# Second-level sums by accumulating DMAs, and a longer lead for loads and splits in the last phase of a Fourier-mixing and gated feed-forward kernel

## The chip, the cores and the metric

The kernel runs on one core of a Trainium2 chip. The metric is the time of one execution on the device in microseconds, the median over several runs; lower is better. The engines are named as in the profile: PE multiplies matrices, PEld loads its weights, DVE and ACT work on vectors, POOL and SP here issue DMAs, and 16 DMA engines move the data.

## The reference, cut to what matters

```python
# x: 1 x 2048 x 640 (S x D); the DFT matrices are 2048 x 2048 and 640 x 640;
# W_gate, W_up: 640 x 1728; W_down: 1728 x 640; all float32
xn = (x - mean(x)) / sqrt(var(x) + 1e-5)                    # over D
a, b = xn @ dft_hid_re.T, xn @ dft_hid_im.T
fnet = dft_seq_re @ a - dft_seq_im @ b
h = relu(xn @ W_gate) * (xn @ W_up)
out = x + fnet + h @ W_down
```

## The kernel before, in words

Every float32 operand is split into a high part of type fp32r and the low remainder, and each product is three matmuls: high times high, high times low, low times high (`mm3`, lines 138 to 140 on PE). A split is two instructions, a copy to the high part on ACT (line 132) and a subtraction on DVE (line 133). To save matmuls, large products are cut into 2 x 2 blocks and done in seven products with sums of blocks (the scheme of Strassen and Winograd).

The kernel has three stages. The first takes the DFT along the sequence, with the matrices streamed in. The second, of 26 steps, makes gate and up, multiplies them, and stores the result `h` in DRAM (`hd`; `hr` is its last 64 rows). Beside that, `pair_weights` prepares the weights of the third stage: it reads two blocks of rows of the hidden DFT matrix or of W_down, makes sums and differences, splits some of them, and POOL stores them in DRAM (`wparts`, `wquads`). The last PE work of this stage is a lead unit on the tile `gw`.

The third stage, `project`, adds both products of the hidden dimension into the output tiles `y`: once for the half q=1 of the sequence, then for q=0. Its unit is one pair (or two) of row blocks times weights. In order, the names of the products are B11, T1, T2, B22 (first part), T3, B22 (rest), T4, with two short B21 units inside T4. Beside them runs a second level (`second_level`) on a part of the output that falls out of the scheme: seven quad products named 1, 2, 5, 6, 3, 7, 4, each over three groups of operands, so 21 quad units. The names 5, 6, 7 and 4 use sums of two blocks.

A unit has steps: `load` (DMAs on SP), `prepare` (sums and splits on DVE and ACT), `run` (PE) and `read` (PE's banks into `y`, on DVE). `drive(4, 2)` walks the list of units: at position i it prepares unit i-2, loads unit i, reads out unit i-5 and runs unit i-4. The order on SP, POOL and PE in this stage is the order of the code; DVE and ACT are ordered by the scheduler. Tiles come from pools with a fixed number of buffers: a DMA into a buffer waits on its queue until the last reader of what stood there before, in this pool or in the space of an earlier one, is done, and all DMAs behind it on that queue wait too.

Names in rows: `rw` and `ro` are blocks of rows of an operand, `wr` is raw weights, `wt` split weights, `cb` a split operand, `q` the second level's operands, `ps` a bank of PE's results, `pq` and `hd` operands in DRAM, `in_hid` and `in_wd` the weights as given.

Of the kernel before, what the change touches and what calls it, by code (L numbers as in the profile page):

```python
# [12 lines left out]
P = 128  # L13
# [18 lines left out]
BACK = 3  # L32

# [20 lines left out]
Z1, Z4, HIGH, LOW, Y21, Y11, Y12 = (2 * P * i for i in (0, 1, 2, 5, 8, 9, 10))  # L54
Z2, Z3, Y22 = (2 * P * i for i in range(3))
NW = 16 * P


QUAD_LOW, QUAD_HIGH, NPREP = 16 * P, 20 * P, 24 * P
QUADS = ((0, 2), (1, 3), (KD, KD + 2), (KD + 1, KD + 3), (KD + 4, KD + 5))  # L60
GROUPS = (("hid", 0, 2, 0), ("f", 0, 2, 2), ("f", 4, 1, 4))
PREP_ORDER = (0, 2, 1, 3, 4, 5, 7, 6, 8, 9, 10)
# [3 lines left out]
def fnet_reglu_kernel(  # L66
# [41 lines left out]
    wquads = dram_p.tile([P, len(QUADS), 4, 2, P], F32, name="wquads")  # L108
# [917 lines left out]
    made = {}  # L1026

    def pair_weights(k, n):

        t = {}  # L1030
        quad = next((i for i, (_, second) in enumerate(QUADS) if second == k), None)

        def load():
            made[k] = t["z"] = z = pool("prep").tile([P, NPREP], F32, name="pw")
            wa, wb = pair(k, 1)
            for w, o1, o2 in ((wa[0], Y11, Y21), (wb[0], Y12, LOW + Y22)):
                rows = slice(0, w.shape[0])
                nc.sync.dma_start(z[rows, o1 : o1 + 2 * P], w[:, : 2 * P])
                nc.sync.dma_start(z[rows, o2 : o2 + 2 * P], w[:, 3 * P :])

        def prepare():
            z = t["z"]
            zz = lambda b: z[:, b : b + 2 * P]
            if k == ODD:
                for o in (Y12, LOW + Y22):
                    nc.vector.memset(z[REST:, o : o + 2 * P], 0.0)
# [7 lines left out]
            if quad is not None:  # L1054
                halves = [[w[:, Y12 + i * P : Y12 + (i + 1) * P] for i in range(2)] for w in (made[QUADS[quad][0]], z)]
                (a11, a21), (a12, a22) = halves
                s1, s2, s3, s4 = (z[:, QUAD_LOW + i * P : QUAD_LOW + (i + 1) * P] for i in range(4))
                minus = lambda o, i0, i1: nc.vector.scalar_tensor_tensor(o, i0, -1.0, i1, op0=OP.mult, op1=OP.subtract)
                tt(s1, a22, a21, op=OP.subtract)
                minus(s2, s1, a11)  # L1060
                tt(s3, a11, a21, op=OP.subtract)
                minus(s4, a12, s2)
                low = z[:, QUAD_LOW:QUAD_HIGH]
                split(z[:, QUAD_HIGH:NPREP].bitcast(F32R), low, low)

        def keep():
            z = t["z"]
            nc.gpsimd.dma_start(wparts[:, k], z[:, :NW])
            if quad is not None:
                for v, at in enumerate((QUAD_HIGH, QUAD_LOW)):  # L1070
                    nc.gpsimd.dma_start(wquads[:, quad, :, v], z[:, at : at + 4 * P].rearrange("p (s n) -> p s n", s=4))

        loads[n - 1].append(load)
        besides[n].append(prepare)
        issues[n + 1].append(keep)

# [43 lines left out]
    for i, k in enumerate(PREP_ORDER):  # L1120
        pair_weights(k, 13 + i)
# [27 lines left out]
    for n, b, side in (("wraw", 4, "left"), ("ring2", 3, "left"), ("wts", 5, "left"), ("raws", 20, "left"),  # L1149
# [6 lines left out]
    SINGLE = (2, ODD_AT)  # L1156
    every = range(len(UNITS))
    fixed = [bank() for _ in range(8)]
# [33 lines left out]
    def project(q):  # L1192
# [3 lines left out]
        B = {("a", 0): A[0], ("a", 1): A[1], ("b", 0): Bk[0], ("b", 1): Bk[1], ("c", 0): Bk[0], ("c", 1): Bk[1],  # L1196
             "v1": fixed[7 if q else 4], "v2": fixed[4], "v3": fixed[4]}
# [20 lines left out]
        def unit(name, u, first, last):  # L1218
# [6 lines left out]
            weights = lambda: pool("wts").tile([P, 2, 2, 3 * P], F32R, name="wt")[:, :n]  # L1225

            def load():
                if name == "B11" and (q, u) == (1, 0):
                    return
                kind = {"B11": "B11", "T1": "B12", "T3": "B21"}.get(name)  # L1230
                if kind:
                    get(kind, u)
# [3 lines left out]
                if name == "B11" and ("B11", 0) not in raws:  # L1236
                    get("B11", 0)
                own, sums = [i.rearrange("k p n -> p k n") for i in pair(k0, n)], wparts[:, k0 : k0 + n]
                if short:
                    t["r"] = r = pool("wraw").tile([P, 2, 3 * P], F32, name="wr")[:, 0]  # L1240
                    for at in (upper, lower):
                        if name == "B22":
                            nc.sync.dma_start(r[at, :P], own[1][:, 0, 2 * P : 3 * P])
                            nc.sync.dma_start(r[at, P:], sums[:REST, 0, Z4 : Z4 + 2 * P])
                        else:
                            cs = slice(0, 3 * P) if name == "B21" else slice(3 * P, D)
                            nc.sync.dma_start(r[at, : cs.stop - cs.start], own[1][:, 0, cs])
                    return
                if name in PARTS:
                    t["w"] = w = weights()  # L1250
                    for j in range(n):
                        at = sums[:, j, HIGH:].rearrange("p (v n) -> p v n", v=2)[:, :, PARTS[name] : PARTS[name] + 2 * P]
                        nc.sync.dma_start(w[:, j, :, : 2 * P].bitcast(F32), at)
                    return
                t["r"] = r = pool("wraw").tile([P, 2, 3 * P], F32, name="wr")[:, :n]
                if name in ("B11", "B21"):
                    nc.sync.dma_start(r, own[name == "B21"][:, :, : 3 * P])
                else:
                    z = (Z1, Z4)[name == "B22"]
                    nc.sync.dma_start(r[:, :, :P], own[name == "B22"][:, :, 2 * P : 3 * P])  # L1260
                    nc.sync.dma_start(r[:, :, P:], sums[:, :, z : z + 2 * P])

            def prepare():
# [5 lines left out]
                if short:  # L1269
                    with in_turn():  # L1270
                        src = r("B21" if name == "T4" else name)[upper, 0]
                        if name == "T4":

                            sub(src, src, r("B12")[upper, 0])
# [3 lines left out]
                        t["w"] = w = weights()[:, 0]  # L1278
                        cs = slice(0, 2 * P if name == "T4" else 3 * P)
                        for i, at in enumerate((upper, lower)):  # L1280
                            split(w[at, i, cs], w[at, 1 - i, cs], t["r"][at, cs])
                    return
                with in_turn():
# [13 lines left out]
                    elif name == "T4":  # L1297

                        src = r("B21")
                        sub(src, src, r("B12"))  # L1300
# [4 lines left out]
                    if "r" in t:  # L1305
                        t["w"] = w = weights()
                        split(w[:, :, 0], w[:, :, 1], t["r"])

            def run():
                b, w = t["b"], t["w"]  # L1310
                key, o, row4 = {"B11": ("a", 0, (2 * P, "v1")), "T1": ("b", P, (0, "v2")), "B21": ("c", 0, (2 * P, "v3")),
                                "T2": ("a", 0, None), "B22": ("b", P, (0, "v2")), "T3": ("a", 0, None),
                                "T4": ("a", 0, None)}[name]
                more = name in ("T2", "B22", "T3", "T4")
# [30 lines left out]
            return load, prepare, run  # L1345
# [27 lines left out]
        for name, us in (("B11", every), ("T1", every), ("T2", every), ("B22", every[:4]), ("T3", every),  # L1373
                         ("B22", every[4:]), ("T4", every[:2]), ("B21", SINGLE), ("T4", every[2:])):
            whole = SINGLE if name == "B21" else every
            for u in us:
                l, p, r = unit(name, u, u == whole[0], u == whole[-1])
                step = [(l, p, r, (lambda name: lambda: read(name))(name) if u == whole[-1] else idle)]
                if u == (5 if (q, name) == (1, "B11") else 3) and name in LOADS_Y:
                    step.append(((lambda which: lambda: get_y(q, *which))(LOADS_Y[name]), idle, idle, idle))  # L1380
# [3 lines left out]
    def second_level():  # L1384


        X, Y = {}, {}
        a, x, v = fixed[5:]

        def fetch(t, q, g):  # L1390
            what, k, n, _ = GROUPS[g]
            t[g] = o = pool("quads").tile([P, 2 * n, CH], F32, name=f"q{q}{g}")
            if what == "hid":
                nc.sync.dma_start(o, pqd[2 * q][1][:, k : k + 2 * n])
            else:
                first = 2 * k + 1
                nc.sync.dma_start(o, hd[q][first : first + 4 * n - 1 : 2, :, :CH].rearrange("f p t -> p f t"))

        def unit(name, g):
# [3 lines left out]
            halves = slice(0, n), slice(n, 2 * n)  # L1403
            part = {"5": 0, "6": 1, "7": 2, "3": 3}.get(name)
            second = name in ("2", "3", "4")
            block = {"1": 0, "2": 0, "4": P}.get(name)
            odd = name in ("1", "2", "5", "3")

            def load():
                own = pair(k + n * second, n)[1].rearrange("k p n -> p k n")  # L1410
                t["w"] = w = pool("wts").tile([P, 2, 2, 3 * P], F32R, name="wt")[:, :n]
                if part is not None:
                    for j in range(n):
# [98 lines left out]
```

## Time and profile before

| | |
|---|---|
| median of 3 runs | 1034.08 us (1033.02 to 1037.72) |
| the profiled execution | 1035.23 us, span 1033.5 us |
| PE busy | 1020.2 us, 99% of the span |
| DVE busy | 837.8 us, 81% |
| ACT busy | 457.5 us, 44% |
| third stage on PE | from 734.54 us to about 1029 us |
| PE's granted clock | 1.00 in every stretch |

The profile lists each engine's busy time, groups of instructions by line and operation with the idle time ahead of them and what ended it (written after an arrow), and single instructions with their start and length in microseconds. A matmul is listed with 0.39 us, but they overlap: one begins some 0.23 us after the one before.

### The profile page before, as it was taken

To read this page: it belongs to the slowest core of one execution; us is meant where nothing else is said; L and a number is where in the kernel's file an instruction comes from. 1 tells how busy PE (TensorE), PEld (TensorE's weight loads), DVE (VectorE), ACT (ScalarE), POOL (GpSimd) and SP (SyncE) were. 2 spreads that over 40 slices of the span, in tenths; PEclk is the share of its full clock that TensorE was granted. 3 is DMA by queue.
4 is the path that set the end of the run, shared out by engine and by line. 5 is a ranking of instruction groups with operands and counts; after the bars stand their busy time and mean duration, and the time that the engine had idled before them with its cause. 6 is when DMAs were issued, how large, how long until landed. Compare 5 with 4: busy or idle time off the path is not lost.

```text
span 1033.5 us, 12722 instructions
## 1 busy us (share of the span) xinstructions
PE 1020.2 (99%) x4510; PEld 840.5 (81%) x4510; DVE 837.8 (81%) x1178; ACT 457.5 (44%) x592; POOL 104.8 (10%) x171
## 2 busy tenths in 40 slices
PE   9999999999999999999999999999999989999997
PEld 8888888888888888888888888888887867788886
DVE  7957977979879697687887888886597779896997
ACT  6664452333334444333346444443454344553453
POOL 2000010212200002421110111111000001000001
PEclk9999999999999999999999999999999999999999
DMA  8885744957859567763465577663888778796665
GB/s 328 328 250 186 257 160 127 363 212 251 322 200 361 189 208 222 246 223 133 174 234 171 198 252 255 240 229 123 314 303 298 239 245 270 256 320 211 197 213 188
DMA packets 114767, 245.31 MB, mean 237 GB/s; under 512 B 12688, under 2 KB 63120, under 8 KB 112912
## 3 DMA queue, kind: packets, MB, share of 16 engines
q1 hardware_dynamic: 96320, 171.72, 49.8%
q0 software_dynamic: 17952, 72.36, 19.2%
q8 instruction: 35, 0.57, 0.2%
q10 hardware_dynamic: 432, 0.43, 0.1%
q14 instruction: 28, 0.23, 0.1%
HBM read 185.73 MB, written 57.69 MB: 236 GB/s over the span
## 4 chain that ended last, share of the span: by engine, by line
PE 91%; DVE 4%; DMA 4%; ACT 1%; issue 0%; SPq 0%; ACTq 0%
PE ps L139 29%; PE ps L140 29%; PE ps L138 29%; PE ps L526 3%; DVE cb L133 1%; DMA wt<-wparts 1%; DMA q<-hd 1%; DVE rw L1267 1%; PE ps L555 1%; DVE y L1178 1%; ACT cb L132 1%; DVE wt L133 1%; DMA wr<-in_hid 1%; PE ps L120 1%; DMA wr<-in_wd 0%
## 5 line engine op out<-in xcount | busy, mean ns | idle before, releaser
L139 PE MATMUL ps<-cb,wt 128*128 128x512 f32 (+1 forms) x407 | 158.7, 390 | 2.9 <-DVE cb L133 2.9
L138 PE MATMUL ps<-cb,wt 128*128 128x512 f32 (+1 forms) x407 | 158.4, 389 | 2.1 <-DMA wt<-wparts 2.1
L140 PE MATMUL ps<-cb,wt 128*128 128x512 f32 (+1 forms) x407 | 158.1, 388 | 1.4 <-DVE wt L133 1.4
L132 ACT ACTIVATE cb<-raw 128x1024 fp32r<-128x1024 f32 x64 | 67.8, 1060 | 103.9 <-PE ps L140 94.6
L132 ACT ACTIVATE cb<-rw 128x1024 fp32r<-128x1024 f32 (+1 forms) x73 | 70.9, 975 | 86.2 <-PE ps L140 47.1
L133 DVE TENSOR_TENSOR cb<-raw,cb 128x1024 fp32r<-128x1024 f32 x64 | 78.1, 1221 | 31.5 <-ACT cb L132 31.1
L133 DVE TENSOR_TENSOR cb<-rw,cb 128x1024 fp32r<-128x1024 f32 (+1 forms) x73 | 81.3, 1119 | 25.4 <-ACT cb L132 25.0
L138 PE MATMUL ps<-xs_early,gw 128*128 128x512 f32 x260 | 101.1, 389 | 0.0
L139 PE MATMUL ps<-xs_early,gw 128*128 128x512 f32 x260 | 101.1, 389 | 0.0
L140 PE MATMUL ps<-xs_early,gw 128*128 128x512 f32 x260 | 101.1, 389 | 0.0
L139 PEld LDWEIGHTS ps<-cb,wt 128*128 128x128 f32 x407 | 76.4, 188 | 20.7 <-DVE cb L133 5.3
L138 PEld LDWEIGHTS ps<-cb,wt 128*128 128x128 f32 x407 | 76.4, 188 | 19.6 <-ACT cb L132 2.1
L140 PEld LDWEIGHTS ps<-cb,wt 128*128 128x128 f32 x407 | 76.4, 188 | 17.4 <-DVE wt L133 1.9
L139 PE MATMUL ps<-cb,xs_late 128*128 128x512 f32 x232 | 90.4, 389 | 0.0
L138 PE MATMUL ps<-cb,xs_late 128*128 128x512 f32 x232 | 90.3, 389 | 0.0
L140 PE MATMUL ps<-cb,xs_late 128*128 128x512 f32 x232 | 90.3, 389 | 0.0
L138 PE MATMUL ps<-cb,xs_early 128*128 128x512 f32 x226 | 87.9, 389 | 0.0
L139 PE MATMUL ps<-cb,xs_early 128*128 128x512 f32 x226 | 87.9, 389 | 0.0
L140 PE MATMUL ps<-cb,xs_early 128*128 128x512 f32 x226 | 87.9, 389 | 0.0
L129 ACT ACTIVATE gw<-z 128x1024 fp32r<-128x1024 f32 (+1 forms) x52 | 57.1, 1112 | 36.5 <-PE ps L140 21.0
L129 ACT ACTIVATE u<-ps 128x512 f32<-128x512 f32 x52 | 31.2, 599 | 89.6 <-PE ps L140 77.7
L874 DVE TENSOR_TENSOR gw<-z,gw 128x1024 fp32r<-128x1024 f32 (+1 forms) x52 | 64.7, 1283 | 1.9 <-ACT gw L129 1.8
(208 smaller groups left out, 2034.3 us busy)
## 6 DMA issues: line engine op xcount, KB each, us to landing
raw<-in_dft SPq DMA_DIRECT2D x94, 512.0 KB, 5.4
wt<-wparts SPq DMA_DIRECT2D x70, 256.0 KB, 4.3
z<-in_wgu SPq DMA_DIRECT2D x26, 640.0 KB, 4.2
hd<-ob POOLq DMA_DIRECT2D x26, 512.0 KB, 3.2
wparts<-pw POOLq DMA_DIRECT2D x12, 1024.0 KB, 5.1
rw<-hd SPq DMA_DIRECT2D x24, 512.0 KB, 6.2
tk<-in_dft SPq DMA_DIRECT2D x16, 512.0 KB, 8.8
rw<-pq SPq DMA_DIRECT2D x16, 512.0 KB, 5.8
```

The lines of the kernel that those rows point to most:

```text
L120: nc.tensor.matmul(ps[:, :P], warm, warm, start=True, stop=True)
L129: return nc.scalar.activation(o, i, AF.Copy)
L132: nc.scalar.activation(hi, src, AF.Copy)
L133: return nc.vector.tensor_tensor(lo, src, hi.bitcast(F32), op=OP.subtract)
L138: nc.tensor.matmul(ps, wh, mh, start=first, stop=False, skip_group_check=more)
L139: nc.tensor.matmul(ps, wh, ml, start=False, stop=False, skip_group_check=more)
L140: nc.tensor.matmul(ps, wl, mh, start=False, stop=last, skip_group_check=more)
L526: nc.tensor.matmul(E[0, key], xn_part(n * SG + j, d)[v == 1], b[:, int(v == 2), j], start=False, stop=n % NH == NH - 1 and (j, v) == (SG - ...
L555: nc.tensor.matmul(E[c, key], xn_part(j, d)[v == 1], b[c][0][:, int(v == 2), j], start=j == 0 and v == 0, stop=False)
L874: tt(self.w[:, 1, cs], self.z[:, cs], self.w[:, 0, cs].bitcast(F32), op=OP.subtract)
L1178: nc.vector.tensor_tensor(t, ps, t, op=OP.add)
L1267: sub = lambda o, i0, i1: nc.vector.tensor_tensor(o, i0, i1, op=OP.subtract)
```

## The change: what it does

- **Second level.** The sums of names 5, 6, 7 and 4 are no longer made on DVE (line 1424). Two kept tiles per group (`x`, `h`) hold one block each; when it has been split for its product, POOL issues a DMA that adds the next block from DRAM onto it (line 1444). Before, all four blocks of a group were loaded whole and kept. The 21 quad units stand elsewhere: four after units of B22 in q=1 (it was seven), seven after B11 in q=0 (as before), six after T1 in q=0 (none before) and four after B22 in q=0 (seven before).
- **The walk.** `drive_last` takes the place of `drive(4, 2)`: at position i it prepares unit i-3, loads rows and fetches weights of unit i, reads out unit i-7 and runs unit i-6. There are seven buffers of weights for five, four of split operands for three, 23 of rows for 20.
- **Weights.** The pool of raw weights is gone. Weights land in the low half of their `wt` tile and are split in place. `wparts` holds all the pieces side by side, so the three pieces of a unit are one DMA with longer rows. The quads' weights are made in units of their own at steps 4, 5, 6, 9 and 10 of the second stage, not with pairs at steps 14 to 24.
- **B21.** The two short units stand behind the B22 units 0 and 1 for q=1, behind 4 and 5 for q=0, with PE banks of their own; before, both stood after the second unit of T4.

```diff
-Z1, Z4, HIGH, LOW, Y21, Y11, Y12 = (2 * P * i for i in (0, 1, 2, 5, 8, 9, 10))
+Z1, O1, Y11, Z4, O2, Y12 = (P * i for i in (0, 2, 3, 5, 7, 8))
+HIGH, LOW, NW, NPREP = 10 * P, 16 * P, 22 * P, 24 * P
...
-    for i, k in enumerate(PREP_ORDER):
-        pair_weights(k, 13 + i)
+    for k in range(ODD):
+        pair_weights(k, 13 + k)
+    for i, n in enumerate((4, 5, 6, 9, 10)):
+        quad_weights(i, n)
...
-    for n, b, side in (("wraw", 4, "left"), ("ring2", 3, "left"), ("wts", 5, "left"), ("raws", 20, "left"),
+    for n, b, side in (("wts", AHEAD + 1, "left"), ("ring2", 4, "left"), ("raws", 23, "left"),
...
+    SINGLE_AFTER = ((("B22", 4), ("B22", 5)), (("B22", 0), ("B22", 1)))
+    QUADS_AFTER = [(1, "B22", u) for u in every[3:]] + [(0, "B11", u) for u in every] + [(0, "T1", u) for u in every[:6]] + [(0, "B22", u) for u in every[:4]]
...
+                first = {"B11": O1, "T1": Z1, "B21": O2, "B22": Z4}[name]
...
-                z = (Z1, Z4)[name == "B22"]
-                nc.sync.dma_start(r[:, :, :P], own[name == "B22"][:, :, 2 * P : 3 * P])
-                nc.sync.dma_start(r[:, :, P:], sums[:, :, z : z + 2 * P])
+                    put(w[:, :, 1], sums[:, :, first : first + 3 * P])
...
-                    if "r" in t:
-                        t["w"] = w = weights()
-                        split(w[:, :, 0], w[:, :, 1], t["r"])
+                    if name not in PARTS:
+                        w = t["w"]
+                        split(w[:, :, 0], w[:, :, 1], w[:, :, 1].bitcast(F32))
...
-                    if name in "5674":
-                        which, half = {"5": (Y, lo), "6": (Y, hi), "7": (Y, hi), "4": (X, hi)}[name]
-                        plus(src, which[g][:, half])
                     t["b"] = b = pool("ring2").tile([P, 2, SG, CH], F32R, name="cb")[:, :, :n]
                     lows.append(split(b[:, 0], b[:, 1], src))
+                    if more is not None:
+                        nc.gpsimd.dma_start(grown[g], block(more[0], g, more[1]), accum_op=OP.add)
...
+    def drive_last():
+
+        n = len(todo)
+        for i in range(n + AHEAD + 2):
+            now[0] = i
+            for f in deferred.pop(i, ()):
+                f()
+            for step, behind in ((1, AHEAD - READY), (4, 0), (0, AHEAD - ROWS), (3, AHEAD + 1), (2, AHEAD)):
+                if 0 <= i - behind < n:
+                    todo[i - behind][step]()
...
-        drive(4, 2)
+        drive_last()
```

How this moves the instructions is shown at two places. The first is SP at the passage from the second to the third stage: the last load of the gate and up weights (`z`), then the first loads of the third stage. Before:

```order
L854 DMA z<-in_wgu 128x1280
L1214 DMA rw<-pq_88 128x1024 x2
L1257 DMA wr<-in_hid 128x2x384
L1214 DMA rw<-pq_88 128x512
L1257 DMA wr<-in_hid 128x384
L1216 DMA rw<-hd_91 128x2x512
L1257 DMA wr<-in_wd 128x2x384
```

And with the change:

```order
L854 DMA z<-in_wgu 128x1280
L1251 DMA wt<-wparts 128x2x384
L1223 DMA rw<-pq_88 128x1024 x2
L1251 DMA wt<-wparts 128x384
L1223 DMA rw<-pq_88 128x512
L1251 DMA wt<-wparts 128x2x384
L1225 DMA rw<-hd_91 128x2x512
```

The weights of the first unit now go ahead of its rows. In both, the second of the two `rw` loads in a row goes into the highest buffer of the pool of rows. With 20 buffers that pool ends below the space of the tile `gw`; with 23 its highest buffer (bytes 167936 to 172032 of a partition) lies over the first bytes of `gw` (from 170496), which the lead unit reads. That second `rw` load, and with it everything behind it on SP, so waits for the last matmul of the lead unit; before, it waits for the last matmul that used an earlier tile at that place.

The second place is DVE around the names 5 and 6 of the second level. Before, with the sums on line 1424:

```order
L1424 TENSOR_TENSOR q_6182<-q_6182,q_6485 128x1024
L133 TENSOR_TENSOR cb<-rw,cb 128x1024 x2
L133 TENSOR_TENSOR wt<-wr,wt 128x2x384
L133 TENSOR_TENSOR cb<-q_6182,cb 128x1024
L133 TENSOR_TENSOR wt<-wr,wt 128x2x128
L133 TENSOR_TENSOR wt<-wr,wt 128x2x384
L133 TENSOR_TENSOR cb<-rw,cb 128x1024
L1178 TENSOR_TENSOR y_6802<-ps,y_6802 128x512
L1178 TENSOR_TENSOR y_6804<-ps,y_6804 128x512
L1424 TENSOR_TENSOR q_6214<-q_6214,q_6522 128x512
```

With the change, from the split for name 5 of the first group (`x_6305`) to that for name 6:

```order
L133 TENSOR_TENSOR cb<-x_6305,cb 128x1024
L133 TENSOR_TENSOR wt<-wt 128x2x128
L133 TENSOR_TENSOR wt<-wt 128x384
L1187 TENSOR_TENSOR y_5801<-ps,y_5801 128x512
L133 TENSOR_TENSOR cb<-rw,cb 128x1024
L1187 TENSOR_TENSOR y_5807<-ps,y_5807 128x512
L133 TENSOR_TENSOR cb<-x_6500,cb 128x1024
L133 TENSOR_TENSOR cb<-ro,cb 128x512
L133 TENSOR_TENSOR wt<-wt 128x128
L133 TENSOR_TENSOR wt<-wt 128x2x384
L133 TENSOR_TENSOR cb<-x_6535,cb 128x512
```

The adds are gone from DVE; the splits read a tile onto which POOL's DMA has added. On POOL those DMAs stand among the stores of finished `y` tiles:

```order
L1199 DMA out<-y_6667 128x512
L1444 DMA x_6305<-pq_86 128x1024
L1199 DMA out<-y_5801 128x512
L1199 DMA out<-y_5807 128x512
L1444 DMA x_6500<-hd_90 128x2x512
L1444 DMA x_6535<-hd_90 128x512
L1444 DMA x_6305<-pq_88 128x1024
```

Before, POOL has only the stores there.

More of the change, by code (lines that the diff above doesn't have):

```diff
@@ L32 @@
 BACK = 3
+AHEAD = 6
 B11, B12, B21, B22, T1, T2, T3, T4, X4 = range(9)
@@ L1224, in unit @@
             t = {}
-            weights = lambda: pool("wts").tile([P, 2, 2, 3 * P], F32R, name="wt")[:, :n]
             def load():
-                if name == "B11" and (q, u) == (1, 0):
-                    return
                 kind = {"B11": "B11", "T1": "B12", "T3": "B21"}.get(name)
-                if kind:
+                if kind and (kind, u) not in raws and (name, q, u) != ("B11", 1, 0):
                     get(kind, u)
@@ L1235, in load @@
                     get("B22", ahead)
-                if name == "B11" and ("B11", 0) not in raws:
+                if (q, name, u) == (1, "B11", 1):
                     get("B11", 0)
-                own, sums = [i.rearrange("k p n -> p k n") for i in pair(k0, n)], wparts[:, k0 : k0 + n]
-                if short:
[L1240 to L1248, printed above, removed]
@@ L1249, in load @@
-                if name in PARTS:
-                    t["w"] = w = weights()
[L1251 to L1257, printed above, removed]
-                else:
-                    z = (Z1, Z4)[name == "B22"]
-                    nc.sync.dma_start(r[:, :, :P], own[name == "B22"][:, :, 2 * P : 3 * P])
-                    nc.sync.dma_start(r[:, :, P:], sums[:, :, z : z + 2 * P])
+                if q and name == "T2" and u in (1, 5):
+                    get("B21", SINGLE[u // 5])
@@ L1384, in second_level, with block @@
     def second_level():
-        X, Y = {}, {}
+        X, H = {}, {}
         a, x, v = fixed[5:]
-        def fetch(t, q, g):
+        def block(q, g, half):
             what, k, n, _ = GROUPS[g]
-            t[g] = o = pool("quads").tile([P, 2 * n, CH], F32, name=f"q{q}{g}")
             if what == "hid":
[L1394 to L1397, printed above, removed]
+                return pqd[2 * q][1][:, k + half * n : k + half * n + n]
+            first = 2 * (k + half * n) + 1
+            return hd[q][first : first + 2 * n - 1 : 2, :, :CH].rearrange("f p t -> p f t")
         def unit(name, g):
```

190 lines of the change are left out of this document (111 added, 79 removed).

## The prediction

> **What bounds the kernel now.** I read the page's totals first, then its groups of PE, then the waits and the stretches of the third stage, and last single instructions around the gaps.
>
> ```profile
> PE 1020.2 (99%) x4510; PEld 840.5 (81%) x4510; DVE 837.8 (81%) x1178; ACT 457.5 (44%) x592; POOL 104.8 (10%) x171
> ...
> DMA packets 114767, 245.31 MB, mean 237 GB/s; under 512 B 12688, under 2 KB 63120, under 8 KB 112912
> ```
>
> PE is the bound; 4510 matmuls in 1020.2 us are one per 0.226 us. The order shows the same matmuls afterwards, so only gaps between them can be won, and new gaps are the only loss. The waits of the third stage (740 us to the end; us in total, times, longest) and its stretches show what gaps there are:
>
> ```profile
> PE ps L139 <- DVE cb L133: 2.9, 5, 0.9
> PE ps L138 <- DMA wt<-wparts: 2.1, 3, 1.5
> PE ps L1321 <- DVE wt L133: 2.1, 2, 1.4
> PE ps L140 <- DVE wt L133: 1.4, 1, 1.4
> ```
>
> ```profile
> 520.00:620.00 100.00, 100.00 (x443) 82.81 (x442) 81.83 (x139) 48.22 (x63) 9.51 (x16) 1.00 0.63 215
> 740.00:780.00 40.00, 40.00 (x178) 33.14 (x177) 34.62 (x39) 18.07 (x22) 0.00 (x0) 1.00 0.93 328
> 820.00:860.00 40.00, 36.52 (x157) 28.87 (x157) 30.74 (x37) 17.44 (x25) 2.75 (x5) 1.00 0.81 260
> 900.00:940.00 40.00, 39.23 (x173) 32.12 (x172) 35.62 (x41) 20.23 (x25) 0.00 (x0) 1.00 0.82 282
> 980.00:1020.00 40.00, 38.94 (x171) 31.57 (x170) 38.08 (x49) 20.93 (x30) 2.53 (x5) 1.00 0.76 238
> ```
>
> The columns are the stretch, its length, then busy time of PE, PEld, DVE, ACT and POOL, the granted clock, the DMA engines' share and GB/s. The second stage leaves PE no gap (520 to 620). The clock is 1.00 throughout, so it explains nothing. The gaps lie in the third stage: 3.5 us of 40 at 820, where DVE has room (30.74 of 40), and a little at 980, where DVE is almost full (38.08 of 40).
>
> **What the gaps are worth.** Two of them, as PE's instructions:
>
> ```profile
> 796.18 0.39 PE L139 MATMUL ps<-cb,wt 128*128 128x512 f32 x1
> 797.92 0.50 PE L140 MATMUL ps<-cb,wt 128*128 128x512 f32 x1 [1.35 <-DVE wt L133]
> ...
> 835.89 0.39 PE L140 MATMUL ps<-cb,wt 128*128 128x512 f32 x1
> 837.80 0.47 PE L138 MATMUL ps<-cb,wt 128*128 128x512 f32 x1 [1.51 <-DMA wt<-wparts]
> ```
>
> From start to start the first takes 1.74 us where 0.226 is the rule: 1.51 lost, 0.16 more than the idle time listed, because an undisturbed matmul overlaps the next by 0.39 - 0.226. So each wait costs its idle time plus 0.16. The four rows hold 2.9 + 2.1 + 2.1 + 1.4 = 8.5 us in 11 waits; with 11 x 0.16 that is 10.3 us.
>
> Do they all go? The one at 835.89 waits for a `wt` whose DMA was issued four units ahead, but behind loads that wait for buffers on the same queue; it and the `L1321` waits are the two short B21 units inside T4, of half the PE time or less and with the same number of instructions on DVE. Now weights are issued six units ahead into two more buffers, splits are made three ahead, and the B21 units stand apart. The waits for `cb` have DVE behind them, and there the change takes work away:
>
> ```profile
> L1424 DVE TENSOR_TENSOR q<-q,q x6: 679/1216/1217, 845.7 to 893.8; 128x1024 f32<-128x1024 f32 x4, 128x512 f32<-128x512 f32 x2
> L1424 DVE TENSOR_TENSOR q<-q x6: 680/1216/1225, 958.2 to 1001.2; 128x1024 f32<-128x1024 f32 x4, 128x512 f32<-128x512 f32 x2
> ```
>
> Twelve adds: 8 x 1.216 + 4 x 0.68 = 12.4 us, of which half lay ahead of the full stretch at 980. Three quad units also leave that end for T1. I take all 10.3 us as gone; what is late next there is DVE's `y` adds, which this change leaves. If a third stays, 3.4 us less.
>
> **The passage into the third stage.** The second `rw` load now waits for the lead unit, and all of SP behind it. Before, the same queue ran so:
>
> ```profile
> 726.57 0.33 SPq L1214 DMA_DIRECT2D rw<-pq  x1
> ...
> 727.41 0.47 SPq L1214 DMA_DIRECT2D rw<-pq  x1
> 727.92 0.43 SPq L1257 DMA_DIRECT2D wr<-in_hid  x1
> 728.40 0.43 SPq L1216 DMA_DIRECT2D rw<-hd  x1
> ```
>
> ```profile
> 734.31 0.39 PE L140 MATMUL ps<-gw 128*128 128x512 f32 x1
> 734.54 0.39 PE L138 MATMUL ps<-cb,wt 128*128 128x512 f32 x1
> ...
> 738.62 0.39 PE L138 MATMUL ps<-cb,wt 128*128 128x512 f32 x1
> ```
>
> ```profile
> 734.24 0.69 DVE L133 TENSOR_TENSOR cb<-rw,cb 128x512 fp32r<-128x512 f32 x1
> 735.03 0.56 DVE L133 TENSOR_TENSOR wt<-wr,wt 128x384 fp32r<-128x384 f32 x1
> 737.09 1.23 DVE L133 TENSOR_TENSOR cb<-rw,cb 128x1024 fp32r<-128x1024 f32 x1 [1.49 <-ACT cb L132]
> ```
>
> The lead unit's last matmul starts at 734.31, so this load is freed at 734.7, about 8.1 us after 726.57. The first unit's data stand ahead of it on SP and are there in time, so PE starts it at 734.54 as before and is free for the second unit (one block of 128x512) at 738.62. That unit's weights and rows are the next two DMAs, issued at 735.2 and 735.7. Before, 7.7 us passed from the issue of its last DMA (727.92) to the end of its split (735.03 + 0.56): that gives 743.4, a gap of 4.8 us. At the other end, a landing in the 3.7 us of the fastest `rw` load there and only the splits of one block (some 1.3 us) give 740.7, a gap of 2.1:
>
> ```profile
> DMA to landing us min/median/max: 3.7/6.3/8.0
> ```
>
> The third unit's 512 KB are issued at 736.6; 9.9 us, as before from 728.40 to 737.09 + 1.23, would make it 746.5 against the 745.4 (743.4 plus nine matmuls) at which PE could take it, 1.1 more. So 2.1 to 5.9; I take 3.5, nearer the lower end, because SP's queue stood idle for eight microseconds and finds the DMA engines emptier than before. From the fourth unit on, one unit of 18 matmuls is 4.1 us of PE for 0.9 MB of loads; the lead is caught up.
>
> **The DMA work.** The second level reads 15 blocks of 256 KB more than before: five in each of four names are added (5.24 MB), and three fives are still loaded where four were. Twelve adding DMAs come on POOL. In full stretches the DMA engines move about 350 GB/s (328 / 0.93 at 740; 282 / 0.82 at 900 gives 344). The tight place is T1 of q=0, which now has six quads: by the order, 153 matmuls, 34.6 us; 10.3 MB of loads (2.36 weights, 4.46 rows, 1.64 quads' weights, 1.31 `h` tiles, 0.52 `y`) and 1.57 MB added. If adding costs what copying does, 11.9 MB are 33.9 us: just full. No adding DMA is in the trace of before. By what it has to do (fetch the operand, fetch the sum, write it) it costs one to two copies; at two it is 38.4 us, 3.8 over. B11 of q=0 has 168 matmuls, 38.0 us, and 8.45 MB plus 2.36 added: 30.9 us at one, 37.6 at two, which fits. Against the 3.8 stands the lead: a step of T1 is 34.6 / 13 = 2.7 us, six are 16.0, less a landing and some 3.2 us for splits.
>
> ```profile
> rw<-hd SPq DMA_DIRECT2D x24, 512.0 KB, 6.2
> ...
> DMA to landing us min/median/max: 8.1/8.4/10.3
> ```
>
> The first row is the page's landing of 512 KB, the second that of the second level's own loads before (tile `q`). With 6.2 there are 6.6 us to spare and nothing is lost; with 10.3, 2.5 are left and 1.3 lost. I take 1.3 of 0 to 3.8.
>
> The Trainium skill, "Collectives: The Full Stack", section "The bandwidth ceiling: the fold count and why AG ≠ RS ≠ AR", says that a reducing DMA is slower not for its add but for its two source reads, with a measured ratio of 1.93. No run here shows it yet, and its case is a ring between cores. With 1.93 the shortfall in T1 would be 3.5 us and the sum the one with two copies; by the row of plain loads alone it would be none.
>
> **At nothing.** Splitting in place is as many instructions as before, and merged weight DMAs are fewer. The making of the quads' weights is moved: five times four sums and a split, under 2.3 us by the 0.69 above for 128x512 and less for the smaller ones, into second-stage steps in which DVE is 82% busy; a step is some 12 us, so some 2 us lie free, and before they stood beside the pair's own work in one step, which PE survived. If that cover is gone, 0.3 us in each of five steps, 1.5 in all. The larger `wparts` (5 MB more) meets a DMA share of 0.63. On POOL an adding DMA stands behind stores of `y` that wait for their last add on DVE; those are a few DVE instructions ahead of it. The last `y` adds and stores after the last matmul stay, and cost the same.
>
> **The sum.** 1035.23 (the profiled execution) - 10.3 + 3.5 + 1.3 = 1029.7. The median is 1.15 below the profiled execution, so in its terms 1034.1 - 5.5 = 1028.6.
>
> **Rivals.**
> - *Adding DMAs far slower than two copies: slower than before.* A name's tile is added to and split again three quads and three units later: for 5 then 6, 12 + 12 + 6 matmuls and 42 of units, 16 us. That cover holds for landings of 16 us, 2.6 times 6.2. Engine time decides earlier: at four copies B11 needs 51.1 us against 38.0 and T1 47.3 against 34.6, 25.8 over, less 6.6 of lead: 19, so 1027.3 + 19 = 1046. Above 1039.3 (0.5%) it lies from about 3.4 copies on. Against it speaks that the operation has three accesses; for it, that software-issued queues show no adding DMA in this trace at all.
> - *Two copies, and landings late as well: no change.* All 3.8 lost, a third of the gaps kept, the passage at 5.9: 1034.1 - 6.9 + 5.9 + 3.8 = 1036.9; with half of these excesses, 1032.
> - *All of the transfers hidden and the passage short.* 1034.1 - 10.3 + 2.1 = 1025.9; if the small delays after each gap go too (about 0.1 each), 1024.5. For it: DMA shares of 0.76 to 0.82 with loads six ahead.
>
> **How the numbers follow.** My forecast 0.42, hidden transfers 0.13, two copies with late landings 0.20, slow adding DMAs 0.25. 0.5% is 5.2 us, about what a measurement can tell: below 1028.9 and above 1039.3. The forecast's own range, 1025.9 to 1031.5, has two thirds below 1028.9 (0.27); with the second-to-last rival's 0.13, faster has 0.41; slower takes 0.25 and 0.02 of the other; the rest, 0.32, is the same. The range leaves out what lies under 1024 and the slow half of the last case: 1024 to 1043.
>
> **What would show it.** After: no wait for `wt<-wparts` and none on B21's line on PE past 800 us; a new gap of 2 to 5 us at 738.6 and perhaps one behind it, waiting for `wt` or `cb` with a DMA behind; in q=0's T1 a DMA share above 0.9; 12 adding DMAs on POOL that land in 6 to 12 us; DVE 12 us less busy. I am wrong if the adding DMAs land in over 16 us, if PE waits for splits of `x` or `h`, or if gaps show in the second stage.

## The result: no gain, and some 0.5% slower

The changed kernel took 1040.28 us (median of 8, 1036.3 to 1041.92) against 1034.34 us for the kernel before in the same runs: a ratio of 1.0047, with an interval of 1.0027 to 1.0067. The forecast of 1028.6 us named the wrong side. Its profiled execution took 1038.57 us, with a span of 1036.8 us, 3.3 us more than that of before. The medians differ by more, 5.9 us: the profile is one of the faster executions of the changed kernel, whose four slowest (1040.75 to 1041.92) show a granted clock of 0.994 to 0.996 against 0.997 or 0.998 in the others. What follows accounts for the 3.3 us; the rest was not profiled.

The page of the changed kernel, its totals and its groups of PE:

```profile
PE 1022.3 (99%) x4510; PEld 843.7 (81%) x4510; DVE 824.5 (80%) x1162; ACT 455.5 (44%) x588; POOL 111.6 (11%) x178
...
DMA packets 111152, 257.08 MB, mean 248 GB/s; under 512 B 12720, under 2 KB 57712, under 8 KB 109552
...
L139 PE MATMUL ps<-cb,wt 128*128 128x512 f32 (+1 forms) x407 | 159.6, 392 | 5.5 <-DVE cb L133 5.5
L138 PE MATMUL ps<-cb,wt 128*128 128x512 f32 (+1 forms) x407 | 159.6, 392 | 3.9 <-ACT cb L132 3.9
```

The matmuls are the same 4510, DVE has 13.3 us less to do, and the DMAs move 11.8 MB more. Of the four kinds of wait before, three are gone: none for `wt<-wparts`, none on the B21 line. In their place stand 9.4 us of waits for `cb`, the split operand. The stretches (columns as in the prediction) show where. First two of before that the prediction doesn't show:

```profile
780.00:820.00 40.00, 38.65 (x170) 31.43 (x169) 28.19 (x33) 18.27 (x23) 0.00 (x0) 1.00 0.74 245
860.00:900.00 40.00, 39.46 (x173) 31.86 (x173) 34.59 (x44) 18.75 (x26) 2.16 (x4) 1.00 0.82 265
```

Then those of the changed kernel:

```profile
740.00:780.00 40.00, 36.70 (x151) 29.50 (x152) 33.49 (x38) 20.17 (x25) 0.00 (x0) 0.96 0.98 358
780.00:820.00 40.00, 40.00 (x179) 33.11 (x178) 32.88 (x40) 18.29 (x23) 0.91 (x1) 1.00 0.74 227
820.00:860.00 40.00, 40.00 (x178) 33.15 (x177) 34.43 (x40) 18.07 (x23) 4.88 (x7) 1.00 0.97 290
860.00:900.00 40.00, 39.25 (x174) 32.17 (x172) 22.74 (x30) 18.37 (x26) 5.23 (x7) 1.00 0.94 293
900.00:940.00 40.00, 37.26 (x155) 30.16 (x156) 29.12 (x36) 18.11 (x25) 5.89 (x6) 0.96 1.06 316
940.00:980.00 40.00, 38.18 (x169) 31.28 (x168) 35.57 (x41) 19.76 (x25) 0.00 (x0) 1.00 0.66 213
980.00:1020.00 40.00, 40.00 (x178) 33.15 (x177) 35.16 (x44) 18.16 (x24) 2.93 (x6) 1.00 0.87 271
```

The stretches from 780 to 860 and from 980 to 1020, which lost time before, are full now. Time is lost in two places: the passage into the third stage, and T1 of q=0 and what lies around it (gaps from 899 to 943), where the DMA engines' share reaches 1.06 (transfers of two queues that overlap in an engine count twice). In the two stretches that lose most, the granted clock falls to 0.96. In single instructions, PE in T1:

```profile
925.67 0.39 PE L138 MATMUL ps<-cb,wt 128*128 128x512 f32 x1
928.01 0.56 PE L139 MATMUL ps<-cb,wt 128*128 128x512 f32 x1 [1.95 <-DVE cb L133]
928.37 0.63 PE L140 MATMUL ps<-cb,wt 128*128 128x512 f32 x1
928.79 0.63 PE L138 MATMUL ps<-cb,wt 128*128 128x512 f32 x1
929.22 0.63 PE L139 MATMUL ps<-cb,wt 128*128 128x512 f32 x1
```

After the gap, eight matmuls run at a pitch of 0.43 us for 0.226: another 1.6 us. The same follows the gaps of the passage. So a gap has a price of its own behind it, which the idle column doesn't show.

For the whole stage I add, over successive matmuls, the time from start to start less 0.226 us. This counts idle time and half rate alike; a span of some narrower matmuls at the end comes out at -1.0.

| lost on PE, us | passage, 734 to 760 | 760 to 880 | T1 and around, 880 to 946 | 946 to the end |
|---|---|---|---|---|
| before | 0.1 | 7.9 | 1.3 | 2.6 |
| changed | 6.8 | 0.3 | 8.2 | -1.0 |

Between 760 and 880 us and at the end 10.5 us of losses became -0.7: 11.2 won. The passage and T1 lost 13.6 us more (6.8 less 0.1, 8.2 less 1.3). Up to 734 us the two differ by another 0.5. That makes 2.9 of the 3.3 us by which the span grew; the rest lies behind the last matmul.

### The profile page after: what moved, and what is told of

Read it like the earlier page. It is cut to its first block, busy times and chain, and to the rows that moved or that the text cites. A ratio compares the mean times of both kernels' runs of the same rounds, so it can differ in the third digit from the quotient of the medians.

```text
span 1036.8 us, 12740 instructions
## 1 busy us (share of the span) xinstructions
PE 1022.3 (99%) x4510; PEld 843.7 (81%) x4510; DVE 824.5 (80%) x1162; ACT 455.5 (44%) x588; POOL 111.6 (11%) x178
## 4 chain that ended last, share of the span: by engine, by line
PE 95%; DMA 3%; DVE 1%; SPq 0%; issue 0%; ACT 0%; ACTq 0%
PE ps L139 30%; PE ps L140 30%; PE ps L138 30%; PE ps L526 3%; DMA rw<-hd 2%; DMA wt<-wparts 2%; PE ps L555 1%; PE ps L1330 1%; PE ps L120 1%; DVE cb L133 0%; ACT cb L132 0%; SPq L1251 0%; SPq L1427 0%; DVE wt L133 0%; ACT wt L132 0%
## 5 line engine op out<-in xcount | busy, mean ns | idle before, releaser
L139 PEld LDWEIGHTS ps<-cb,wt 128*128 128x128 f32 x407 | 77.3, 190 | 23.0 <-DVE cb L133 7.2
L138 PEld LDWEIGHTS ps<-cb,wt 128*128 128x128 f32 x407 | 77.3, 190 | 21.2 <-ACT cb L132 5.3
L140 PEld LDWEIGHTS ps<-cb,wt 128*128 128x128 f32 x407 | 77.0, 189 | 15.9
L133 DVE TENSOR_TENSOR wt<-wt 128x768 fp32r<-128x768 f32 (+5 forms) x64 | 44.7, 714 | 35.7 <-ACT wt L132 35.2
```

The lines of the kernel that those rows point to most:

```text
L133: return nc.vector.tensor_tensor(lo, src, hi.bitcast(F32), op=OP.subtract)
L138: nc.tensor.matmul(ps, wh, mh, start=first, stop=False, skip_group_check=more)
L139: nc.tensor.matmul(ps, wh, ml, start=False, stop=False, skip_group_check=more)
L140: nc.tensor.matmul(ps, wl, mh, start=False, stop=last, skip_group_check=more)
```

## The experiments

Each edit is to the changed kernel unless said otherwise; losses are from the profiled execution, times are medians. The kernel before was timed again with each group of runs, with medians from 1034.19 to 1035.42 us, so about 1 us between runs of different groups shows nothing. First the two new losses, each undone alone and then together.

**22 buffers of rows.**

```diff
-    ... ("raws", 23, "left"),
+    ... ("raws", 22, "left"),
```

> The changed kernel with 22 buffers of rows for 23, so that the pool of rows ends below the tile that the lead unit reads. Theory (the loads behind the lead unit are late because SP stands behind one load whose buffer lies over that tile): SP issues the third stage's loads some 8 us earlier, the gaps of 5.2 us at 738 to 747 us and the eight matmuls at half rate after them (1.6 us) are gone, and the time falls by some 6.8 us, to about 1033.5 us; the 8.0 us lost between 898 and 945 us stay. Rival (the DMA engines are backed up there anyway, or one buffer fewer makes later loads wait): gaps of over 3 us stay at that place or new ones come, and the time stays above 1037 us.

Measured: 1034.97 us, ratio 0.9995 (0.9984 to 1.0006). The passage loses 0.1 us instead of 6.8, so the mechanism holds: SP stood behind the load over the lead unit's tile. But T1 lost 11.3 us in this execution instead of 8.2, and the time fell by 5.3, not 6.8. Its DMA engines had no more room there than before (share 1.04).

**Plain copies in place of adding DMAs.**

```diff
-   nc.gpsimd.dma_start(grown[g], block(more[0], g, more[1]), accum_op=OP.add)
+   nc.gpsimd.dma_start(grown[g], block(more[0], g, more[1]))
```

> The changed kernel with its twelve adding DMAs made plain copies of the same blocks from the same queue; the sums of the second level are left out. Theory (adding costs the DMA engines about two copies, and that makes the loads of T1 late): the DMA share between 900 and 940 us falls from 1.06 to about 0.95, the 8.0 us lost between 898 and 945 us fall to under 3, and the time falls by 5 us or more, to about 1035 us. Rival (it is not the add but the place, six quads and their loads beside T1): the losses there stay above 6 us and the time at about 1040 us.

Measured: 1031.99 us, ratio 0.998 (0.9967 to 0.9993). The loss in T1 fell from 8.2 to 3.8 us and the share between 900 and 940 from 1.06 to 0.98. The add is the larger part (4.4 of 8.2), but not all: "under 3" was missed.

**Quads beside T2 for T1.**

```diff
- + [(0, "T1", u) for u in every[:6]] +
+ + [(0, "T2", u) for u in every[:6]] +
```

> The changed kernel with the six quads that stand beside T1 of q=0 moved beside T2 of q=0, where the DMA share is 0.66 (940 to 980 us); the adding DMAs stay. Theory (T1 with its rows loaded ahead has no room in the DMA engines): the 8.0 us lost between 898 and 945 us fall to under 3, T2 takes the extra transfers without a gap of over 1 us, the time falls by 5 us or more, to about 1035 us. Rival (adding DMAs are late wherever they stand, because their own tile is needed again too soon): the gaps wander to T2 and PE waits for splits of x or h there; the time stays within 2 us of 1040.

Measured: 1033.87 us, ratio 0.9988 (0.9976 to 0.9999). T1 and around lost 2.4 us, the end 0.9 for -1.0. So the six quads cost most of what T1 loses where the DMA engines are already full, and little where they aren't. The edit moves their loads along with their adds and doesn't part the two.

**Both.** The two edits with 22 buffers and with T2, together.

> 22 buffers of rows and the six quads beside T2. Theory: both gains add, some 6.8 and 6 us: about 1027.5 us, 0.6% below the kernel before. Rival (with the first gaps gone, the queue reaches the next tight place earlier and loses there): no better than the better of the two single edits, about 1033 us.

Measured: 1027.57 us, ratio 0.9929 (0.9914 to 0.9944). The two gains add as expected; the rival falls.

Next, what the adding DMA itself brings, and what closed the old gaps.

**Sums on DVE, 22 buffers, quads beside T1.** SP loads the block to be added into a buffer of rows, six steps ahead; DVE adds it.

```diff
+                if name in ADDED:
+                    t["add"] = pool("raws").tile([P, 2, CH], F32, name="rw")[:, :n]
+                    nc.sync.dma_start(t["add"], block(ADDED[name][0], g, ADDED[name][1]))
...
+                    if name in ADDED:
+                        nc.vector.tensor_tensor(src, src, t["add"], op=OP.add)
...
-                    if more is not None:
-                        nc.gpsimd.dma_start(grown[g], block(more[0], g, more[1]), accum_op=OP.add)
```

> 22 buffers of rows, quads beside T1 as in the change, but the second level's sums made on DVE: SP loads the block to be added into a buffer of rows six steps ahead, DVE adds it before the split. As many bytes are read as with adding DMAs. To be compared with 22 buffers and adding DMAs (1034.97 us; 8.7 us lost between 890 and 945 us). Theory (an adding DMA costs about two copies): the DMA share between 900 and 940 us falls below 1.0, the loss there falls to under 5 us, as with plain copies, and the time to about 1031 us. Rival (DVE's 12.4 us of adds cost more than the DMA engines' extra work): waits for cb take their place and the time is 1035 us or more.

Measured: 1023.5 us, ratio 0.9889 (0.9871 to 0.9907): the fastest of all, and 11.5 us better than the same kernel with adding DMAs. The theory had 1031 us and a DMA share below 1.0 between 900 and 940 us; the share is 1.00, and the gain far larger. The third stage has no gap over 0.15 us left. Its PE total and its fullest stretches:

```profile
PE 1016.6 (100%) x4510; PEld 841.4 (82%) x4510; DVE 835.2 (82%) x1174; ACT 456.1 (45%) x588; POOL 99.6 (10%) x166
```

```profile
900.00:940.00 40.00, 40.00 (x178) 33.10 (x178) 37.13 (x45) 18.27 (x24) 0.00 (x0) 1.00 1.00 347
940.00:980.00 40.00, 40.00 (x178) 33.14 (x177) 37.55 (x44) 20.08 (x26) 0.54 (x1) 1.00 0.78 249
```

Between 900 and 940 us DVE is 93% busy and the DMA engines are full, and PE waits for neither; the engines move 347 GB/s there, where the changed kernel moved 316 at a share of 1.06. The adds that the change took off DVE had cost nothing there.

**Sums on DVE, quads beside T2.** The same edit on the version with both.

> 22 buffers of rows and six quads beside T2 (1027.57 us with adding DMAs), with the sums on DVE as in the run before. Theory (adding DMAs hurt only where the DMA engines are full, and beside T2 they are not): within 2 us of 1027.6; the gaps left at 893 (B11) shrink, those at 946 to 951 grow, since DVE is busy there. Rival (adding DMAs are what the change loses by, everywhere): 1025 us or less.

Measured: 1026.74 us, ratio 0.992 (0.9904 to 0.9936): 0.8 us better than with adding DMAs, no clear difference, as the theory had it. Beside T2, an adding DMA does little harm; but with the sums on DVE, T1 is the better place for the quads by 3.2 us.

**The old lead with adding DMAs.** On the version with both:

```diff
-AHEAD = 6
+AHEAD = 4
...
-    READY, ROWS = 3, 6
+    READY, ROWS = 2, 4
```

> 22 buffers of rows and six quads beside T2, with the lead of the kernel before: loads four steps ahead, splits two (with five buffers of weights). Theory (the lead is what removed the old gaps): gaps of 1 to 2 us come back at waits for weights and cb, 8 us or more in all, and the time rises to about 1036 us. Rival (fewer adds, the fourth cb buffer and the B21 units' new places removed them): no more than 2 us slower, under 1030 us.

Measured: 1046.42 us, ratio 1.0106 (1.0078 to 1.0134), 18.9 us worse than with the lead of six. Twice the 8 us or more expected.

**Quads spread wider.** On the version with both:

```diff
- ... + [(0, "B11", u) for u in every] + [(0, "T2", u) for u in every[:6]] + [(0, "B22", u) for u in every[:4]]
+ ... + [(0, "B11", u) for u in (1, 3, 5)] + [(0, "T2", u) for u in every] + [(0, "B22", u) for u in every[:4]] + [(0, "T3", u) for u in (0, 2, 4)]
```

> 22 buffers of rows; the quads spread wider: three beside B11 of q=0 for seven, seven beside T2 for six, three beside T3 that had none. Theory (what is left, 1.3 us at 893 and 2 us at 946 to 951, comes from too many quads' transfers beside B11 and T2): the gap at 893 goes, the time falls by 1 to 2 us, to about 1026 us. Rival (T3, with DVE's last sums and y adds, has no room): new gaps after 980 us, 1028 us or more.

Measured: 1036.2 us, ratio 1.0017 (1.0002 to 1.0032). Both expectations missed: nothing new after 980 us, but one gap of 6.2 us that ends at 947, in T2. The chain of waits of this kernel has there

```profile
934.82 11.23 DMA h<-pq
946.12 0.26 issue
946.38 1.05 ACT cb L132
```

a load of `h` by SP that landed after 11.23 us. Why this one took so long was not followed up.

**The old lead with sums on DVE.** The fastest version, with `AHEAD` 4 and `READY, ROWS` 2, 4 as above.

> The version with sums on DVE, 22 buffers of rows and quads beside T1 (1023.5 us, no gap over 0.15 us in the third stage), with the lead of the kernel before: loads four steps ahead, splits two, five buffers of weights. With adding DMAs the short lead cost 19 us. Theory (the short lead hurt there because adding DMAs make every landing late; with plain loads it costs what the kernel before lost at waits for weights, some 4 us): about 1028 us, waits for weights come back. Rival (the lead by itself is what closed the gaps): 10 us or more, 1033 us and above.

Measured: 1041.51 us, ratio 1.0061 (1.0043 to 1.0079), 18.0 us more than with the lead of six; 12.0 us are lost in T1. The theory fell, the rival's time holds: the lead counts, with plain loads as with adding ones. But the short lead doesn't bring the old gaps back where they were: between 760 and 880 us it loses 2.0 us, where the kernel before lost 7.9; most of its losses are in T1, where the kernel before, with the same lead and no quads, lost 1.3.

**The short B21 units of q=0 back inside T4.** On the fastest version:

```diff
-    SINGLE_AFTER = ((("B22", 4), ("B22", 5)), (("B22", 0), ("B22", 1)))
+    SINGLE_AFTER = ((("T4", 1), ("T4", 1)), (("B22", 0), ("B22", 1)))
```

> The same version with the two short B21 units of q=0 again behind the second unit of T4 (q=1 stays as changed, since its banks are taken there). Theory (the B21 units inside T4 caused the gaps of 0.9 and 0.7 us with DVE full near the end): 1 to 2 us slower, about 1025 us, with gaps after 1000 us on PE. Rival (fewer adds on DVE and the longer lead are enough): within 0.5 us of 1023.5.

Measured: 1023.9 us, within 0.5 of 1023.5, and no gap. For q=0 the new place gained nothing once the lead is there. The B21 units of q=1, beside which the larger old gaps stood (836 and 840 us), were not moved back.

**Three buffers of split operands.** On the fastest version:

```diff
-    ... ("ring2", 4, "left"), ...
+    ... ("ring2", 3, "left"), ...
```

> The same version with three buffers of split operands for four. Theory (with splits three steps ahead, a fourth buffer is needed, since three are taken by units that wait): the lead in splits falls back to two and gaps at waits for cb come, 1 to 4 us: about 1026 us. Rival (three are enough where no landing is late): 1023.5.

Measured: 1029.55 us, 6 us more, with waits for `cb` throughout (2.0, 2.2 and 1.6 us in the three later columns of the table, the last for -1.0). More than expected; a split three steps ahead needs the fourth buffer.

**23 buffers of rows on the fastest version.**

```diff
-    ... ("raws", 22, "left"),
+    ... ("raws", 23, "left"),
```

> The same version with 23 buffers of rows, so that SP again waits for the lead unit. Theory (the passage costs its 5.2 us of gaps and, where PE's clock drops behind them, 1.6 us, whatever comes later): 1028.5 to 1030.5 us, gaps at 738 to 747 only. Rival (most of it was made good later, since T1's DMAs get a later start): under 1027 us.

Measured: 1028.9 us, 5.4 us more; 4.7 us lost at the passage, no new loss elsewhere. So the passage's price is not made good later. In the profile it is lower than in the changed kernel (4.7 against 6.8 us).

Three more runs asked what exactly in T1 was late.

**The blocks to be added loaded early, but by POOL.** On the fastest version:

```diff
-                    nc.sync.dma_start(t["add"], block(ADDED[name][0], g, ADDED[name][1]))
+                    nc.gpsimd.dma_start(t["add"], block(ADDED[name][0], g, ADDED[name][1]))
```

> The version with sums on DVE (1023.5 us), its twelve blocks to be added loaded by POOL instead of SP, still six steps ahead. Theory (it is the late issue, behind the split of the tile, that costs; not the queue): within 0.7 us of 1023.5, under 1 us lost in T1. Rival (transfers of POOL's queue take turns with SP's in the DMA engines and delay the weights): 2 us or more lost in T1, 1026 us or more.

Measured: 1026.65 us, 3.2 us more than by SP; 2.2 us lost in T1 and 1.6 before. The rival's numbers hold: the loads cost without a late issue too. But POOL issued the loads at other times than SP. Five of them go out within 4 us, ahead of T1:

```profile
882.69 0.54 POOL L1427 DMA_DIRECT2D rw<-pq  x1
883.39 1.27 POOL L1427 DMA_DIRECT2D rw<-hd  x2 [0.16 <-issue]
884.65 0.53 POOL L1427 DMA_DIRECT2D rw<-pq  x1
886.18 0.71 POOL L1427 DMA_DIRECT2D rw<-hd  x1 [1.00 <-issue]
```

SP had issued the same five between 879.5 and 917.2 us. Whether the queue itself costs or this clump is not shown.

**22 buffers of rows, with plain copies.** The first two edits together; the second level's sums are left out again.

> 22 buffers of rows, adding DMAs made plain copies at the same place (sums of the second level left out). To be compared with adding DMAs (1034.97 us, 11.3 us lost between 880 and 946 us) and with sums on DVE (1023.5 us, 0.3 us lost). Theory (two copies' worth of engine time per add is most of it): 3 to 4 us lost there, about 1027.5 us. Rival (most of it is the place of issue): over 6 us lost, above 1030 us.

Measured: 1026.88 us, 8.1 us less than with adding DMAs on the same base and 3.4 more than with SP's loads and sums on DVE. T1 and around loses 1.8 us, less than the 3 to 4 expected. So of 11.5 us, 8.1 go with the adding; the other 3.4 are about what issuing the loads from POOL cost in the run before. The DMA queues between 890 and 945 us (q1 is SP's, q0 POOL's; packets, MB, share of the 16 engines), first with 22 buffers and adding DMAs:

```profile
q1 hardware_dynamic: 9647, 14.35, 73.4%
q0 software_dynamic: 1234, 2.82, 28.0%
```

then with copies (this run):

```profile
q1 hardware_dynamic: 11117, 16.07, 83.7%
q0 software_dynamic: 736, 2.62, 13.2%
```

In MB per per cent of share SP's queue moves 0.196 and 0.192. POOL's moves 0.198 when it copies and 0.101 when it adds: an added byte takes the engines 0.196 / 0.101 = 1.94 times as long as a copied one (1.9 to 2.0 with the two other copies' figures).

**A lead of five.** `AHEAD` 5 and `READY, ROWS` 3, 5 on the fastest version.

> The version with sums on DVE, with loads five steps ahead for six, splits three ahead as they are, six buffers of weights. With six it loses 0.3 us in T1, with four (splits two ahead) 12. Theory (no reserve: what a load and its splits need is already the whole lead where the DMA engines are full): 4 to 8 us lost in T1, 1028 to 1033 us. Rival (the lead of six held a reserve of about 6.6 us, more than two steps): under 1 us lost, at most 1024.5 us.

Measured: 1025.66 us, 2.2 us more than with six; T1 loses 1.9 us. Neither expectation holds: there is a little reserve in six steps, less than one step of 2.7 us, not 6.6.

## Why the prediction was wrong, point by point

**The old gaps, 10.3 us won: right in size, the cause only in part.** All of them went (7.9 us between 760 and 880, and those at the end). The prediction gave three reasons: the longer lead, the place of the B21 units, and DVE's twelve adds. The adds were no reason: with them back on DVE no gap comes back. The B21 units of q=0 were none either (0.4 us). The lead and the fourth `cb` buffer are needed (18 and 6 us without them), but without either only some 2 of the 7.9 us between 760 and 880 come back. What closed the rest of those gaps stays open; the B21 units of q=1 and the merged weight DMAs were not undone.

**The passage, 3.5 us taken from 2.1 to 5.9: right mechanism, too small.** It measured 6.8 us here, and 5.3 us in the median. SP of the changed kernel runs as worked out:

```profile
735.17 0.32 SPq L1223 DMA_DIRECT2D rw<-pq  x1
735.54 0.42 SPq L1251 DMA_DIRECT2D wt<-wparts  x1
736.01 0.43 SPq L1223 DMA_DIRECT2D rw<-pq  x1
736.49 0.43 SPq L1251 DMA_DIRECT2D wt<-wparts  x1
736.96 0.47 SPq L1225 DMA_DIRECT2D rw<-hd  x1
```

```profile
740.90 0.50 PE L138 MATMUL ps<-cb,wt 128*128 128x512 f32 x1 [1.68 <-ACT cb L132]
...
745.13 0.50 PE L138 MATMUL ps<-cb,wt 128*128 128x512 f32 x1 [1.42 <-ACT cb L132]
746.39 0.51 PE L139 MATMUL ps<-cb,wt 128*128 128x512 f32 x1 [0.76 <-DVE cb L133]
```

The second unit lost 2.5 us, close to the lower end. The third lost 2.7, where I had added 1.1 at most: its 512 KB, last of five DMAs issued within 1.8 us, landed after 7.04 us, by the chain of waits:

```profile
736.96 7.04 DMA rw<-hd
744.02 1.07 ACT cb L132
745.11 1.24 DVE cb L133
```

I had let the second unit's delay stand for the third's. The gaps alone, 5.2 us, lie inside the range and 1.7 above the value taken. The 1.6 us at half rate were not in the sum at all.

**The DMA work, 1.3 us taken from 0 to 3.8: this term failed.** An adding DMA does cost about two copies, 1.94, the end of my range from which 3.8 us came. But T1 and around lost 8.2 us, 6.9 more than the value taken. Two things were wrong. The reserve of 6.6 us was worked out from a median landing of 6.2 us, while PE's wait is set by the latest landing: the median of the 512 KB loads of `hd` from 890 to 945 us was 6.8, but those in the chain of waits took up to 11.89. The chain there, with the start and the time from issue to landing:

```profile
889.08 9.08 DMA wt<-wparts
...
913.68 11.89 DMA rw<-hd
...
932.42 6.71 DMA wt<-wparts
```

From SP's release at 910.9 us to PE's matmul at 928.0 the second of these took 17.1 us, where the prediction had a lead of 16.0: 2.8 for the issues ahead of it on SP, for which the sum had no term, 11.9 to land, 2.4 for a sum and a split. The split for which PE waited there is of an `h` tile, a sign of being wrong that the prediction named:

```profile
925.60 1.23 DVE L1274 TENSOR_TENSOR rw<-rw 128x1024 f32<-128x1024 f32 x1 [2.13 <-DMA rw<-hd]
926.74 1.22 DVE L133 TENSOR_TENSOR cb<-h,cb 128x1024 fp32r<-128x1024 f32 x1
```

The tile itself was there, since ACT began to copy it at 922.38 us, but DVE stood at the sum ahead of its split, and the sum waited for the late rows.

And B11, which I let fit at two copies, left the engines no room before T1 began, since their share was already 0.94 from 860 to 900; this was not tested alone. The run with a lead of five shows how little was in hand. Then half rate added 1.6 us of the 8.2.

The Trainium skill, "Collectives: The Full Stack", section "The bandwidth ceiling: the fold count and why AG ≠ RS ≠ AR", gave 1.93 for a reducing against a copying transfer, measured in a ring of cores. Here a DMA that adds from DRAM onto a tile took 1.94 times a copy's engine time. The two agree to within the 1.9 to 2.0 above; what the ratio does to a kernel that is full at that place did not follow from it.

**At nothing.** The moved quads' weights cost nothing that shows: up to 734 us the two executions differ by 0.5 us, with DVE 86% busy between 500 and 600. POOL's order cost nothing visible; twelve loads issued from POOL did, 3.2 us.

**The rivals.** The one nearest to what happened is the second, two copies and late landings, with a fifth of the chance; of its parts only the old gaps did not stay. (Half of its excesses of 8.3 us over 1028.6 gives 1032.8, not 1032.) The rival that ended slower asked for 3.4 copies or more; two suffice where the lead holds hardly any reserve.

## What to carry to other kernels

Taking work off an engine that isn't the bound, and handing it to one that is full in that very stretch, can be a loss, as here: look at the DMA engines' share where the transfers will run, not at its mean. Count a lead as reserve only after taking off the longest landing seen with the engines full, not the median. When a pool grows, look at what its highest buffer now overlaps: one load that waits for old data holds up its whole queue.

## What was not expected of the hardware

- After some gaps of PE, eight matmuls ran at half rate (a pitch of 0.43 us): behind gaps of 2.1 us at 925.7, and of 1.6 and 1.0 us at 743 to 746. A gap of 2.0 us at 941 was not followed by any. The Trainium skill, "TensorE: Matmul & The Clock Gate", section "What's actually happening", tells of a free-running window of some 3.4 us by which the clock is halved; eight matmuls at 0.43 us are 3.4 us, which agrees, and a gap shorter than the window was enough here. The traces show more: the clock is 0.50 for stretches of 3.41 us, and in the same time ahead of the two in the changed kernel PE was busy for only 1.51 and 1.46 us. The gap at 941 fell into two such stretches, of which the emptier had 2.06. Ahead of the half rate in T1, during it, and behind the gap at 941:

```profile
924.90:928.31 3.41, 1.46 (x7) 0.92 (x6) 2.64 (x3) 1.26 (x2) 0.00 (x0) 1.00 1.06 397
928.32:931.72 3.40, 3.40 (x9) 2.67 (x8) 3.17 (x6) 1.68 (x3) 1.39 (x2) 0.50 1.04 399
941.97:945.37 3.40, 2.06 (x9) 1.72 (x10) 3.40 (x5) 1.06 (x1) 0.00 (x0) 1.00 1.08 391
```

So, by these figures, whether a gap is followed by half rate depends also on where it falls; no run was made to test this.

- Loads issued by POOL instead of SP, of the same blocks at the same steps of the walk, cost 3.2 us (1026.65 against 1023.5), although a copied byte took the same engine time on both queues (0.198 and 0.192). Five of them went out in a clump; whether that or the queue delays the others stays open.
